# Two column halves for the last subtile, and a new order of loads, masks and attention items at the start of a fused attention and MLP kernel

## Chip, cores, metric

One Trainium2 chip, one core. The metric is the device time in microseconds (us) of one execution. Runs of a kernel mostly agree within 0.3 per cent; a few are in a slower state and left out of the ratios.

Names: TensorE (PE; PEld is its weight load), VectorE (DVE), ScalarE (ACT), GpSimd (POOL), SyncE (SP). A "q" after a name (PEldq, DVEq) marks that engine's sequencer, under which the profile lists branches, semaphore instructions and the issuing of DMAs; it can be ahead of the engine itself (in the kernel before, TensorE's reaches its branch at 305.5 us, and TensorE's last matmul ends at 308.97). A semaphore is a counter by which engines wait for one another. PSUM is the memory that the matmuls of this kernel write to; a bank is a part of it.

## The reference

```python
def reference(q, k, v, s, w_in, w_out):             # q, k, v: (8, 8, 576, 64)
    scores = q @ k^T / 8, causal mask, plus min(-(cum_i - cum_j), 0), cum = cumsum(max(s, 0))
    x = softmax(scores) @ v                          # -> (4608, 512): 8 batches of 576 tokens
    return gelu(x @ w_in) @ w_out                    # 512 -> 2048 -> 512, exact gelu
```

## The kernel before

The MLP runs over nine chunks of 512 tokens. A chunk has layer 1 (8 steps of two feature tiles; in the first chunk 16 steps, because its two token halves are done one after the other), then layer 2 in four subtiles of 128 tokens. The attention of the next batch is slotted in between. A filler is a matmul on zeros whose result nobody reads. A flag `bad`, computed from the data in an earlier chunk, decides whether a slow general path must redo everything; with this data it never does, but the branch is there. The last subtile of the last chunk is stored only behind the branch.

```python
    def l2_item(c, subs, f0=0, f1=FT, store=True):
        ...
        for ft in range(f0, f1):
            for sub in subs:
                nc.tensor.matmul(y_of[c, sub], lhsT=gT[:, ft, sub*128:(sub+1)*128],
                                 rhs=w_out_r[:, ft, :], start=(ft == 0), stop=(ft == FT - 1))
        if f1 == FT and store: ...                   # copy to SBUF, store
    ...
    load_v(0, nc.gpsimd, (0, 1)); load_w(0, 0); load_w(0, 1)      # one statement a line in the kernel
    load_v(0, nc.gpsimd, (2, 3)); load_w(0, 2); load_w(0, 3)
    scale_v(0, 1, nc.gpsimd)
    ...                                              # first scores, masks, attention items
            late = [                                 # what follows each of the 16 steps of chunk 0's layer 1
                [], [], [], [(av, 0, 0, 2), (av, 0, 1, 2)], [(av, 0, 0, 3)],
                [(av, 0, 1, 3), (to_xT, 0, 2, True)], [(to_xT, 0, 3, True)],
                [(scale_v, 0, 4), (av, 0, 0, 4)],
                [(av, 0, 1, 4), (to_xT, 0, 4, True)],
            ] + [[]] * 7
    ...
            for sub in range(4):                     # layer 2 of the last two chunks
                l2_item(c, (sub,), store=(c, sub) < LAST)
    fast.close()
    rv = nc.values_load(bad[0:1, 0:1], min_val=0, max_val=1)
    with tc.If(rv > 0):
        ...                                          # general path; ends with the last subtile anew
    with tc.manual_schedule():
        ...                                          # last subtile: columns 0:256 by VectorE, stored by SyncE,
                                                     # columns 256:512 by ScalarE, stored by ScalarE
```

Of the kernel before, what the change touches and what calls it, by code (L numbers as in the profile page):

```python
# [19 lines left out]
def kernel(  # L20
# [10 lines left out]
    nc = tc.nc  # L31
# [10 lines left out]
    ST = 5  # L42
# [195 lines left out]
        nc.scalar.activation(cum, s_pos, func=AF.Identity, scale=-1.0, bias=s_pos[:, 287:288])  # L238

    def weights():  # L240
        t_ps = ps.tile([128, ST, BH], fp32, tag="av", bufs=2, name="t_ps")
        for st in range(ST):
            n_st = 128 if st < ST - 1 else SL
            nc.tensor.transpose(
                t_ps[:n_st, st, :], cum[:, st * 128 : st * 128 + n_st], ident[:64, :64]
            )
        nc.scalar.activation(wb[:, 0 : ST - 1], t_ps[:, 0 : ST - 1], func=AF.Exp, scale=-1.0)
        nc.scalar.activation(wb[:SL, ST - 1], t_ps[:SL, ST - 1], func=AF.Exp, scale=-1.0)
# [46 lines left out]

    def cert_2():
        g = cg[0]
        g_ps = ps.tile([3, 128], fp32, tag="av", bufs=2, name="cg_ps")
        nc.tensor.transpose(g_ps, g, ident)
        g3 = const.tile([3, 1], fp32, name="cg3")  # L300
        nc.vector.tensor_reduce(g3, g_ps, axis=AX, op=ALU.max)

        cg[1] = g33 = const.tile([3, 3], fp32, name="cg33")
        nc.vector.tensor_scalar(g33, ident[:3, :3], g3, None, op0=MULT)

    def cert_3():
        g33 = cg[1]
        h_ps = ps.tile([64, 3], fp32, tag="av", bufs=2, name="ch_ps")
        nc.tensor.matmul(h_ps, lhsT=ones[:3, :64], rhs=g33, start=True, stop=True)
        h = const.tile([64, 3], fp32, name="ch")  # L310
        nc.vector.tensor_copy(h, h_ps)
        m = const.tile([64, 1], fp32, name="cm")
        nc.vector.tensor_tensor(m, h[:, 0:1], h[:, 1:2], op=MULT)

        f = const.tile([64, 1], fp32, name="cf")
        nc.vector.tensor_scalar(f, m, -2.0 * D * scale / 256, 1.0, op0=MULT, op1=ALU.add)
        nc.vector.tensor_scalar_max(f, f, 0.0)
        for _ in range(8):
            nc.vector.tensor_tensor(f, f, f, op=MULT)
        nc.vector.tensor_scalar(keep, keep, f, None, op0=MULT)  # L320
        nc.vector.tensor_tensor(goods[:, 6:9], drop, keep, op=ALU.is_le)
        le(goods[:, 9:10], m, MAX_SC / (D * scale))
        le(goods[:, 10:11], h[:, 2:3], 50.0**2)
        le(goods[:, 11:12], h[:, 2:3], 1e-6, ALU.is_ge)

    def cert_4():

        n_ps = ps.tile([1, 12], fp32, tag="av", bufs=2, name="cn_ps")
        nc.tensor.matmul(n_ps, lhsT=ones[:64, 0:1], rhs=goods, start=True, stop=True)
        n = const.tile([1, 1], fp32, name="cn")  # L330
        nc.vector.tensor_reduce(n, n_ps, axis=AX, op=ALU.min)
        le(n, n, 63.5)
        nc.vector.tensor_copy(bad, n)
# [67 lines left out]
    def to_xT(b, it, pe=False):  # L401
        n = 128 if it < ST - 1 else SL
        t0 = b * S + it * 128
        x = x_of[b, it]
        if not pe:
            nc.sync.dma_start_transpose(out=xT[:, :, t0 : t0 + n], in_=x[:n, :])
            return
        t_ps = ps.tile([128, NP, 128], bf16, tag="av", bufs=2, name="xt_ps")
        for p in range(NP):
            nc.tensor.transpose(  # L410
                t_ps[:, p, :n], x[:n, p * 128 : (p + 1) * 128], ident_bf[:n, :n]
            )
        nc.vector.tensor_copy(xT[:, :, t0 : t0 + n], t_ps[:, :, :n])  # L413
# [8 lines left out]

    def idle(n):

        f_ps = ps.tile([128, 256], fp32, tag="av", bufs=2, name="i_ps")
        for _ in range(n):
            nc.tensor.matmul(f_ps, lhsT=zero[:, :128], rhs=zero[:, :256], start=True, stop=True)

    def av_item(b, g, it, later=False):
        P = P_of[b, g]  # L430
        n = 128 if it < ST - 1 else SL
        o_ps = ps.tile([128, 4, D + 1], fp32, tag="av", bufs=2, name="av")
        for h in range(4):
            for i, (jt, off) in enumerate(BLK[it]):
                nc.tensor.matmul(  # L435
                    o_ps[:, h, :],
                    lhsT=P[:, h, off : off + 128],
                    rhs=vv[b % 2][:, jt, 4 * g + h, :],
                    start=(i == 0), stop=(i == len(BLK[it]) - 1),
                )  # L440
        if g == 0:
            x_of[b, it] = work.tile([128, H * D], bf16, tag="x", bufs=6, name="x")
        rc = work.tile([128, 4], fp32, tag="rc", bufs=3, name="rc")
        nc.vector.reciprocal(rc[:n], o_ps[:n, :, D])  # L444
        nc.vector.tensor_tensor(  # L445
            x_of[b, it][:n, g * 256 : g * 256 + 256].rearrange("p (h d) -> p h d", d=D),
            o_ps[:n, :, 0:D],
            rc[:n].unsqueeze(2).to_broadcast([n, 4, D]),
            op=MULT,
        )  # L450
        if g == HG - 1 and b > 0 and not later:
            to_xT(b, it)
# [20 lines left out]
            gT_of[c][:, f2 * 2 : f2 * 2 + 2, n0:n1], h_ps, func=AF.Gelu  # L473
        )

    def l2_item(c, subs, f0=0, f1=FT, store=True):
        gT = gT_of[c]
        if f0 == 0:
            for sub in subs:
# [1 line left out]
        for ft in range(f0, f1):  # L481
            for sub in subs:
# [1 line left out]
                    y_of[c, sub], lhsT=gT[:, ft, sub * 128 : (sub + 1) * 128], rhs=w_out_r[:, ft, :],  # L484
                    start=(ft == 0), stop=(ft == FT - 1),
                )
        if f1 == FT and store:
            for sub in subs:
                o_sb = ost.tile([128, KO * 128], fp32, tag="osb", bufs=3, name="o_sb")
                if c == 0:  # L490
                    nc.scalar.activation(o_sb, y_of[c, sub], func=AF.Copy)
                else:
                    nc.vector.tensor_copy(o_sb, y_of[c, sub])  # L493
                r0 = c * NB + sub * 128
                nc.sync.dma_start(out=out[r0 : r0 + 128, :], in_=o_sb)
# [24 lines left out]
    load_v(0, nc.gpsimd, (0, 1))  # L520
    load_w(0, 0)
    load_w(0, 1)
    load_v(0, nc.gpsimd, (2, 3))
    load_w(0, 2)
    load_w(0, 3)
    scale_v(0, 1, nc.gpsimd)
    load_v(0, nc.gpsimd, (4,))
    load_qks(1)
    load_w(1, 0)
# [14 lines left out]
    scale_v(0, 0)  # L544
    sc_first(1, 0, (1,), 0)
    av_item(0, 0, 0)
    av_item(0, 0, 1)
    mk_item(0, 1, 0, 0, 2)
    sc_first(0, 1, (1,))
    mk_item(0, 1, 0, 2, 4)  # L550
    sc_first(1, 1, (0,), 0)
    av_item(0, 1, 0)
    av_item(0, 1, 1)
    sc_first(1, 1, (1,), 0)
    to_xT(0, 0, True)
    filler(1)
    to_xT(0, 1, True)
    mk_item(0, 0, 1)
    scale_v(0, 2)
    mk_item(0, 1, 1)  # L560
    scale_v(0, 3)
    gelu_set()

# [6 lines left out]
    for c in range(NCH):  # L570
# [4 lines left out]
        if c == 0:  # L575

            late = [
                [], [], [], [(av, 0, 0, 2), (av, 0, 1, 2)], [(av, 0, 0, 3)],
                [(av, 0, 1, 3), (to_xT, 0, 2, True)], [(to_xT, 0, 3, True)],
                [(scale_v, 0, 4), (av, 0, 0, 4)],  # L580
                [(av, 0, 1, 4), (to_xT, 0, 4, True)],
            ] + [[]] * 7
            for half in range(2):
                for f2 in range(FT // 2):
                    l1_item(0, f2, half * 256, half * 256 + 256)
# [69 lines left out]
                    groups(c, (sub,), side[4 * sub : 4 * sub + 4])  # L655
        else:
            for sub in range(4):
                l2_item(c, (sub,), store=(c, sub) < LAST)
                if c == B - 1:
                    (cert_1, cert_2, cert_3, cert_4)[sub]()  # L660
    fast.close()
# [2 lines left out]
    with tc.If(rv > 0):  # L664
        with tc.tile_pool(name="gen", bufs=1) as gen, tc.tile_pool(
# [20 lines left out]
            with tc.For_i(0, B, 1) as b:  # L686
# [8 lines left out]
                for h in range(H):  # L695
# [17 lines left out]
                    for it in range(ST):  # L713
# [22 lines left out]
                        nc.vector.tensor_scalar(den[:n_i], den[:n_i], 1e-9, None, op0=ALU.add)  # L736
                        nc.vector.reciprocal(out=den[:n_i], in_=den[:n_i])
                        nc.vector.tensor_scalar(x[:n_i, :w], x[:n_i, :w], den[:n_i], None, op0=MULT)
                        o_ps = gps.tile([128, 128], fp32, tag="g3", bufs=1, name="go_ps")
                        e = h % 2  # L740
                        h0 = h - e
                        for jt in range(it + 1):
                            n_j = 128 if jt < ST - 1 else SL
                            p_ps = gps.tile([128, 128], fp32, tag="g1", bufs=2, name="gp_ps")
                            nc.tensor.transpose(
                                p_ps[:n_j, :n_i], x[:n_i, jt * 128 : jt * 128 + n_j], ident[:n_i, :n_i]
                            )
# [19 lines left out]
                        )  # L767
                    nc.scalar.activation(g[:, ft, :n], h_ps[:, :n], func=AF.Gelu)

            def layer_2(h_ps, g, sub):  # L770
                for ft in range(FT):
                    nc.tensor.matmul(
                        h_ps, lhsT=g[:, ft, sub * 128 : (sub + 1) * 128], rhs=w_out_r[:, ft, :],
                        start=(ft == 0), stop=(ft == FT - 1),
                    )

# [10 lines left out]
            g = gen.tile([128, FT, NB], bf16, name="gl")  # L787
            layer_1(g, (NCH - 1) * NB, NB)
            for sub in range(LAST[1], 4):
                layer_2(y_of[LAST[0], sub], g, sub)  # L790

    with tc.manual_schedule():
        for sub in range(LAST[1], 4):
            y = y_of[LAST[0], sub]
            r0 = LAST[0] * NB + sub * 128
            for i, (copy, eng) in enumerate(
                [(nc.vector.tensor_copy, nc.sync), (lambda o, a: nc.scalar.activation(o, a, func=AF.Copy), nc.scalar)]  # L797
            ):
                cols = slice(i * 256, i * 256 + 256)
                o_sb = ost.tile([128, KO * 128], fp32, tag="osb", bufs=3, name="o_sb")[:, :256]  # L800
                copy(o_sb, y[:, cols])  # L801
                eng.dma_start(out=out[r0 : r0 + 128, cols], in_=o_sb)


# [28 lines left out]
```

## Time and profile before

| | before |
|---|---|
| time, median of the first three runs | 316.21 us (315.69, 316.21, 320.75) |
| span of the profiled run, TensorE busy in it | 314.2 us, 302.0 us |
| layer 1 of the first chunk starts; layer 2 | 19.46; 36.74 us |
| last matmul ends | 308.97 us |
| VectorE's last copy starts; ScalarE's | 309.48; 309.94 us |
| last store issued (end of the issue) | 310.72 us |

The main lines of the profile before are shown in the prediction. Two more, from its chain of waits (who waited <- for what: us in total, times, longest):

```profile
ACT o_sb L797 <- DVE o_sb L801: 13.7, 1, 13.7
DVE o_sb L801 <- DVEq L664: 3.2, 1, 3.2
```

Line 664 is the branch. ScalarE's last copy waits for VectorE's, and VectorE's waits for its own sequencer at the branch.

### The profile page before, as it was taken

What the parts mean: (1) busy time and instruction counts of PE and PEld (TensorE: products, weight loads), DVE (VectorE), ACT (ScalarE), POOL (GpSimd) and SP (SyncE); (2) the same over time, 40 slices, a digit from 0 to 9 for tenths busy, and PEclk for the clock granted to TensorE, in tenths of its full rate; (3) what the DMA queues carried; (4) which work ended last, traced back from release to release, by engine and by line L of the source; (5) the groups of instructions that cost most, each with busy time, mean ns of one, the idle gap of its engine ahead of it and who ended that gap; (6) DMA issues with size and microseconds to landing.
All of it is one profiled execution on the core that took longest, in us unless ns stands there. A gap on an engine that the chain in (4) does not pass through costs nothing. (4 is left out here: it accounts for less than half of the span.)

```text
span 314.2 us, 6059 instructions
## 1 busy us (share of the span) xinstructions
PE 302.0 (96%) x2475; PEld 155.5 (49%) x2516; DVE 199.0 (63%) x398; ACT 191.0 (61%) x258; POOL 54.5 (17%) x73
## 2 busy tenths in 40 slices
PE   8899999999999999999999999999999999999993
PEld 3477755544554455545454455444544555444441
DVE  7776658599769856975598459955895532250020
ACT  2786878887737673875586658756776666105400
POOL 8653341133001500070007000500000000000000
PEclk9999999999999999999999999999999999999999
DMA  7999999779521973179307951633101331010012
GB/s 124 222 230 209 225 211 270 163 140 211 141 84 25 199 173 102 22 166 206 102 17 171 190 118 36 143 79 91 50 19 42 102 52 26 33 72 32 1 68 75
DMA packets 30979, 36.46 MB, mean 116 GB/s; under 512 B 15648, under 2 KB 20000, under 8 KB 30944
## 3 DMA queue, kind: packets, MB, share of 16 engines
q0 software_dynamic: 11552, 23.07, 38.1%
q1 hardware_dynamic: 19248, 12.80, 14.4%
q8 instruction: 21, 0.34, 0.4%
q14 instruction: 14, 0.11, 0.1%
q10 hardware_dynamic: 144, 0.13, 0.1%
HBM read 36.85 MB, written 9.44 MB: 147 GB/s over the span
## 5 line engine op out<-in xcount | busy, mean ns | idle before, releaser
L483 PE MATMUL o_ps<-w_out_r,gT 128*128 128x512 bf16 x551 | 132.2, 379 | 2.4 <-issue 1.6
L467 PE MATMUL h_ps<-xT,w_in_r 128*128 128x512 bf16 (+1 forms) x625 | 131.4, 357 | 1.3 <-DVE xT L413 0.5
L472 ACT ACTIVATE gT<-h_ps 128x1024 bf16<-128x1024 f32 (+1 forms) x80 | 75.1, 939 | 64.5 <-PE h_ps L467 63.7
L467 PEld LDWEIGHTS <-w_in_r 128*128 128x128 bf16 x640 | 59.8, 98 | 54.2 <-issue 0.6
L483 PEld LDWEIGHTS <-gT 128*128 128x128 bf16 x576 | 51.9, 98 | 56.6 <-issue 3.0
L359 ACT ACTIVATE P<-sc_ps 128x1024 bf16<-128x1024 f32 x56 | 54.3, 1021 | 30.5 <-PE sc_ps L344 30.5
L122 POOL DMA_DIRECT2D raw_v<-in_v_dram x40 | 34.1, 863 | 128.4 <-ACT sq L213 115.7
L493 DVE COPY o_sb<-o_ps 128x512 f32<-128x512 f32 x31 | 21.4, 691 | 46.5 <-PE o_ps L483 46.5
L444 DVE RECIPROCAL rc<-av 128x4 f32<-128x4 f32 (+1 forms) x80 | 14.0, 175 | 39.4 <-PE av L435 39.3
L187 DVE STREAM_TRANSPOSE qkT<-raw_qk 128x576 f32<-128x576 f32 x32 | 37.4, 1242 | 1.8 <-DMA raw_qk<-in_k_dram 1.7
L445 DVE TENSOR_TENSOR x<-av,rc 128x256 bf16<-128x256 f32 (+1 forms) x80 | 33.8, 423 | 3.0
L435 PEld LDWEIGHTS <-P 128*128 128x128 bf16 x576 | 27.1, 97 | 16.5 <-issue 0.8
L205 DVE TENSOR_REDUCE amx<-raw_qk 128x2 f32<-128x2304 bf16 x14 | 35.1, 2532 | 0.0
L435 PE MATMUL av<-vv,P 128*128 128x65 bf16 x576 | 30.5, 193 | 0.6 <-POOL vv L221 0.2
L367 DVE TENSOR_TENSOR P<-P,tri_bf 128x1024 bf16<-128x1024 bf16 (+1 forms) x33 | 22.0, 669 | 9.1 <-ACT P L359 9.1
L221 DVE TENSOR_TENSOR vv<-raw_v,wb 128x512 bf16<-128x512 f32 (+1 forms) x39 | 25.4, 690 | 2.5 <-DMA raw_v<-in_v_dram 2.5
L213 ACT ACTIVATE sq<-raw_v 128x512 bf16<-128x512 f32 (+1 forms) x40 | 24.8, 621 | 0.0
L344 PE MATMUL sc_ps<-qkT 32*128 32x256 bf16 (+2 forms) x560 | 18.2, 250 | 0.0
L344 PEld LDWEIGHTS <-qkT 32*128 32x128 bf16 x560 | 11.7, 92 | 12.4 <-issue 11.6
L498 ACT ACT_TABLE_LOAD x8 | 10.3, 1283 | 0.9 <-PEq L817 0.8
L419 PE MATMUL f_ps<-zero 128*128 128x512 bf16 x26 | 9.3, 494 | 1.2 <-DVE zero L150 1.2
L501 ACT ACT_TABLE_LOAD x8 | 10.3, 1283 | 0.1
(81 smaller groups left out, 92.3 us busy)
## 6 DMA issues: line engine op xcount, KB each, us to landing
out_dram<-o_sb SPq DMA_DIRECT2D x35, 256.0 KB, 2.2
raw_v<-in_v_dram POOLq DMA_DIRECT2D x32, 256.0 KB, 5.5
raw_qk<-in_q_dram POOLq DMA_DIRECT2D x7, 576.0 KB, 7.5
raw_qk<-in_k_dram POOLq DMA_DIRECT2D x7, 576.0 KB, 10.4
w_in_r<-in_moe_w_in_dram POOLq DMA_DIRECT2D x4, 512.0 KB, 12.1
w_out_r<-in_moe_w_out_dram POOLq DMA_DIRECT2D x4, 512.0 KB, 15.8
raw_v<-in_v_dram POOLq DMA_DIRECT2D x8, 128.0 KB, 6.4
raw_qk<-in_q_dram POOLq DMA_DIRECT2D x2, 288.0 KB, 6.2
```

The costliest lines, as they stand in the source:

```text
L122: eng.dma_start(out=t[:n_st, st, :, :], in_=bass.AP(tensor=v.tensor, offset=v.offset + b * H * S * D + st * 128 * D, ap=[[D, n_st], [S * D ...
L187: nc.vector.transpose(qkT[b % 2][:, i, g, :S, :].rearrange("p s e -> p (s e)").bitcast(fp32) .rearrange("p (l j) -> p j l", j=LT), raws[b, ...
L205: nc.vector.tensor_reduce(amx[:, b * HG + g], raws[b, "qk"][:, :, g, :], axis=AX, op=ALU.max, apply_absolute_value=True,)
L213: nc.scalar.activation(sq[:n_st], raws[b, "v"][:n_st, st].rearrange("p h d -> p (h d)"), func=AF.Square, accum_out=sumv[:n_st, b, st : st ...
L221: eng.tensor_tensor(vv[b % 2][:n_st, st, :, 0:D], raws[b, "v"][:n_st, st, :, :], w.unsqueeze(2).to_broadcast([n_st, H, D]), op=MULT,)
L344: nc.tensor.matmul(s_ps[h // 2][:, h % 2, off : off + n], lhsT=qk[r, 1, g, jt * 128 : jt * 128 + 128, e], rhs=qk[r, 0, g, i0 : i0 + n, e], ...
L359: nc.scalar.activation(P[:, 2 * h2 : 2 * h2 + 2, o : o + 512], s_ps[h2], func=AF.Exp, scale=scale)
L435: nc.tensor.matmul(o_ps[:, h, :], lhsT=P[:, h, off : off + 128], rhs=vv[b % 2][:, jt, 4 * g + h, :], start=(i == 0), stop=(i == len(BLK[it ...
L445: nc.vector.tensor_tensor(x_of[b, it][:n, g * 256 : g * 256 + 256].rearrange("p (h d) -> p h d", d=D), o_ps[:n, :, 0:D], rc[:n].unsqueeze( ...
L467: nc.tensor.matmul(h_ps[:, i, :], lhsT=w_in_r[:, ko, ft * 128 : (ft + 1) * 128], rhs=xT[:, ko, c * NB + n0 : c * NB + n1], start=(ko == 0) ...
L472: nc.scalar.activation(gT_of[c][:, f2 * 2 : f2 * 2 + 2, n0:n1], h_ps, func=AF.Gelu)
L483: nc.tensor.matmul(y_of[c, sub], lhsT=gT[:, ft, sub * 128 : (sub + 1) * 128], rhs=w_out_r[:, ft, :], start=(ft == 0), stop=(ft == FT - 1),)
```

## The change

The intent: let ScalarE and VectorE copy the two halves of the last subtile at the same time, from two PSUM banks; start attention items sooner; and take away the waits in the first layer 1 by moving attention items later, while w_in's third quarter lands ahead of value tiles 2 and 3.

```diff
+    def l2_last(c, sub):
+        y_of[c, sub] = []
+        for cols, tag in ((slice(0, 256), "mlp"), (slice(256, 512), "av")):
+            y = yps.tile([128, KO * 128], fp32, tag=tag, bufs=2, name="o_ps")[:, :256]
+            y_of[c, sub].append((cols, y))
+            for ft in range(FT):
+                nc.tensor.matmul(y, lhsT=gT_of[c][:, ft, sub*128:(sub+1)*128], rhs=w_out_r[:, ft, cols],
+                                 start=(ft == 0), stop=(ft == FT - 1))
...
     load_w(0, 1)
-    load_v(0, nc.gpsimd, (2, 3))
     load_w(0, 2)
-    load_w(0, 3)
     scale_v(0, 1, nc.gpsimd)
+    load_v(0, nc.gpsimd, (2, 3))
+    load_w(0, 3)
...
     av_item(0, 0, 0)
+    mk_item(0, 1, 0, 0, 2)
+    sc_first(0, 1, (1,), 0)
     av_item(0, 0, 1)
-    mk_item(0, 1, 0, 0, 2)
-    sc_first(0, 1, (1,))
...                                    # one filler moved; mk_item(0, 1, 1) ahead of scale_v(0, 2)
-                [], [], [], [(av, 0, 0, 2), (av, 0, 1, 2)], [(av, 0, 0, 3)],
-                [(av, 0, 1, 3), (to_xT, 0, 2, True)], [(to_xT, 0, 3, True)],
-                [(scale_v, 0, 4), (av, 0, 0, 4)],
-                [(av, 0, 1, 4), (to_xT, 0, 4, True)],
-            ] + [[]] * 7
+                [], [], [], [], [(av, 0, 0, 2)],
+                [(av, 0, 1, 2), (av, 0, 0, 3)], [(av, 0, 1, 3), (to_xT, 0, 2, True)],
+                [(to_xT, 0, 3, True)], [(scale_v, 0, 4), (av, 0, 0, 4)],
+                [(av, 0, 1, 4)], [(to_xT, 0, 4, True)],
+            ] + [[]] * 5
...
-                l2_item(c, (sub,), store=(c, sub) < LAST)
+                if (c, sub) < LAST: l2_item(c, (sub,))
+                else: l2_last(c, sub)
...                                    # tiles of tag "av" move to the pool that stays open; the general path
                                       # and the last copies take (columns, tile) pairs
```

More of the change, by code (lines that the diff above doesn't have):

```diff
@@ L240, in weights @@
     def weights():
-        t_ps = ps.tile([128, ST, BH], fp32, tag="av", bufs=2, name="t_ps")
+        t_ps = yps.tile([128, ST, BH], fp32, tag="av", bufs=2, name="t_ps")
         for st in range(ST):
@@ L297, in cert_2 @@
         g = cg[0]
-        g_ps = ps.tile([3, 128], fp32, tag="av", bufs=2, name="cg_ps")
+        g_ps = yps.tile([3, 128], fp32, tag="av", bufs=2, name="cg_ps")
         nc.tensor.transpose(g_ps, g, ident)
@@ L307, in cert_3 @@
         g33 = cg[1]
-        h_ps = ps.tile([64, 3], fp32, tag="av", bufs=2, name="ch_ps")
+        h_ps = yps.tile([64, 3], fp32, tag="av", bufs=2, name="ch_ps")
         nc.tensor.matmul(h_ps, lhsT=ones[:3, :64], rhs=g33, start=True, stop=True)
@@ L326, in cert_4 @@
     def cert_4():
-        n_ps = ps.tile([1, 12], fp32, tag="av", bufs=2, name="cn_ps")
+        n_ps = yps.tile([1, 12], fp32, tag="av", bufs=2, name="cn_ps")
         nc.tensor.matmul(n_ps, lhsT=ones[:64, 0:1], rhs=goods, start=True, stop=True)
@@ L407, in to_xT @@
             return
-        t_ps = ps.tile([128, NP, 128], bf16, tag="av", bufs=2, name="xt_ps")
+        t_ps = yps.tile([128, NP, 128], bf16, tag="av", bufs=2, name="xt_ps")
         for p in range(NP):
@@ L423, in idle @@
     def idle(n):
-        f_ps = ps.tile([128, 256], fp32, tag="av", bufs=2, name="i_ps")
+        f_ps = yps.tile([128, 256], fp32, tag="av", bufs=2, name="i_ps")
         for _ in range(n):
@@ L431, in av_item @@
         n = 128 if it < ST - 1 else SL
-        o_ps = ps.tile([128, 4, D + 1], fp32, tag="av", bufs=2, name="av")
+        o_ps = yps.tile([128, 4, D + 1], fp32, tag="av", bufs=2, name="av")
         for h in range(4):
@@ L474, in l1_item, with l2_item @@
         )
-    def l2_item(c, subs, f0=0, f1=FT, store=True):
+    def l2_last(c, sub):
[4 more added lines that the diff above has]
+            for ft in range(FT):
+                nc.tensor.matmul(
+                    y, lhsT=gT_of[c][:, ft, sub * 128 : (sub + 1) * 128], rhs=w_out_r[:, ft, cols],
+                    start=(ft == 0), stop=(ft == FT - 1),
+                )
+    def l2_item(c, subs, f0=0, f1=FT):
         gT = gT_of[c]
@@ L486, in l2_item @@
                 )
-        if f1 == FT and store:
+        if f1 == FT:
             for sub in subs:
@@ L522 @@
     load_w(0, 1)
+    load_w(0, 2)
+    scale_v(0, 1, nc.gpsimd)
     load_v(0, nc.gpsimd, (2, 3))
-    load_w(0, 2)
     load_w(0, 3)
-    scale_v(0, 1, nc.gpsimd)
     load_v(0, nc.gpsimd, (4,))
@@ L546 @@
     av_item(0, 0, 0)
+    mk_item(0, 1, 0, 0, 2)
+    sc_first(0, 1, (1,), 0)
     av_item(0, 0, 1)
-    mk_item(0, 1, 0, 0, 2)
-    sc_first(0, 1, (1,))
     mk_item(0, 1, 0, 2, 4)
     sc_first(1, 1, (0,), 0)
+    filler(1)
     av_item(0, 1, 0)
@@ L555 @@
     to_xT(0, 0, True)
-    filler(1)
     to_xT(0, 1, True)
     mk_item(0, 0, 1)
+    mk_item(0, 1, 1)
     scale_v(0, 2)
-    mk_item(0, 1, 1)
     scale_v(0, 3)
@@ L657 @@
             for sub in range(4):
-                l2_item(c, (sub,), store=(c, sub) < LAST)
+                if (c, sub) < LAST:
+                    l2_item(c, (sub,))
+                else:
+                    l2_last(c, sub)
                 if c == B - 1:
@@ L738 @@
                         nc.vector.tensor_scalar(x[:n_i, :w], x[:n_i, :w], den[:n_i], None, op0=MULT)
-                        o_ps = gps.tile([128, 128], fp32, tag="g3", bufs=1, name="go_ps")
+                        o_ps = gps.tile([128, 128], fp32, tag="g4", bufs=1, name="go_ps")
                         e = h % 2
@@ L743 @@
                             n_j = 128 if jt < ST - 1 else SL
-                            p_ps = gps.tile([128, 128], fp32, tag="g1", bufs=2, name="gp_ps")
+                            p_ps = gps.tile([128, 128], fp32, tag="g1", bufs=1, name="gp_ps")
                             nc.tensor.transpose(
@@ L768, in layer_1, with layer_2 @@
                     nc.scalar.activation(g[:, ft, :n], h_ps[:, :n], func=AF.Gelu)
-            def layer_2(h_ps, g, sub):
+            def layer_2(h_ps, g, sub, cols=slice(0, 512)):
                 for ft in range(FT):
                     nc.tensor.matmul(
-                        h_ps, lhsT=g[:, ft, sub * 128 : (sub + 1) * 128], rhs=w_out_r[:, ft, :],
+                        h_ps, lhsT=g[:, ft, sub * 128 : (sub + 1) * 128], rhs=w_out_r[:, ft, cols],
                         start=(ft == 0), stop=(ft == FT - 1),
@@ L789 @@
             for sub in range(LAST[1], 4):
-                layer_2(y_of[LAST[0], sub], g, sub)
+                for cols, y in y_of[LAST[0], sub]:
+                    layer_2(y, g, sub, cols)
     with tc.manual_schedule():
         for sub in range(LAST[1], 4):
-            y = y_of[LAST[0], sub]
             r0 = LAST[0] * NB + sub * 128
-            for i, (copy, eng) in enumerate(
-                [(nc.vector.tensor_copy, nc.sync), (lambda o, a: nc.scalar.activation(o, a, func=AF.Copy), nc.scalar)]
+            for (cols, y), copy, eng in zip(
+                y_of[LAST[0], sub],
+                (nc.vector.tensor_copy, lambda o, a: nc.scalar.activation(o, a, func=AF.Copy)),
+                (nc.sync, nc.scalar),
             ):
-                cols = slice(i * 256, i * 256 + 256)
                 o_sb = ost.tile([128, KO * 128], fp32, tag="osb", bufs=3, name="o_sb")[:, :256]
-                copy(o_sb, y[:, cols])
+                copy(o_sb, y)
                 eng.dma_start(out=out[r0 : r0 + 128, cols], in_=o_sb)
```

## The prediction

> **What bounds the kernel now.** I read the page first, then the matmul engine's timeline of the first 60 us, GpSimd's timeline (it issues the loads), the landing times of the loads by tile, and last the tail, including the sequencers. The page:
>
> ```profile
> span 314.2 us, 6059 instructions
> PE 302.0 (96%) x2475; PEld 155.5 (49%) x2516; DVE 199.0 (63%) x398; ACT 191.0 (61%) x258; POOL 54.5 (17%) x73
> DMA  7999999779521973179307951633101331010012
> ```
>
> TensorE is busy for 302.0 of 314.2 us; all that any reordering can win is in the other 12.2 us and in filler matmuls. Of these, 1.2 us lie before the first matmul, and 5.2 us after the last one ends (308.97). The third line says more: slices of 7.85 us, so for the first 50 us or so the DMA engines are full. The timeline of GpSimd shows what they are full of, and how each issue is held back by an earlier landing (start, duration, what ended the idle time):
>
> ```profile
> 12.14 0.75 POOL L147 DMA_DIRECT2D w_in_r<-in_moe_w_in_dram  x1 [0.77 <-DMA raw_qk<-in_k_dram]
> 14.05 1.10 POOL L221 TENSOR_TENSOR vv<-raw_v,wb 128x512 bf16<-128x512 f32 x1 [1.17 <-DMA raw_v<-in_v_dram]
> ...
> 26.11 1.55 POOL L147 DMA_DIRECT2D w_out_r<-in_moe_w_out_dram  x2 [1.95 <-DMA w_in_r<-in_moe_w_in_dram]
> ...
> 44.72 0.88 POOL L122 DMA_DIRECT2D raw_v<-in_v_dram  x1 [1.98 <-DMA w_out_r<-in_moe_w_out_dram]
> ```
>
> Counting issues, each one waits for the landing of the one eight before it. With the times from issue to landing I get the order of arrival: w_in quarters 0 and 1 at 16.1 and 18.7, value tiles 2 and 3 at about 19.8 and 20.8, w_in quarter 2 at 23.0 (10.61 + 12.4), quarter 3 at 25.84 (12.14 + 13.7), w_out quarter 2 at 41.0 (26.11 + 14.9), quarter 3 at 44.4 (about 26.9 + 17.5). Now the matmul engine at these moments:
>
> ```profile
> 25.66 0.39 PE L410 MATMUL xt_ps<-ident_bf,x 128*128 128x128 bf16 x4
> 25.88 1.04 PE L467 MATMUL h_ps<-xT,w_in_r 128*128 128x256 bf16 x8
> ...
> 28.25 0.37 PE L435 MATMUL av<-vv,P 128*128 128x65 bf16 x7 [0.20 <-DVE vv L221]
> ...
> 30.46 0.23 PE L410 MATMUL xt_ps<-ident_bf,x 64*128 64x64 bf16 x2 [0.56 <-DVE x L445]
> ...
> 44.57 1.03 PE L483 MATMUL o_ps<-w_out_r,gT 128*128 128x512 bf16 x4
> ```
>
> The step of layer 1 that needs w_in quarter 3 (the seventh, two feature tiles a step) starts at 25.88, 0.04 us after that quarter lands. The layer 2 group that needs w_out quarter 3 (the seventh of eight) starts at 44.57, some 0.15 us after its landing. So the head of this kernel is already in step with the stream of loads: TensorE shows almost no idle time there, but it has almost no room to be earlier either.
>
> The tail, from the rows of the branch that guards the general path, and the end of the timeline:
>
> ```profile
> L664 DVEq COMPARE_BRANCH  x1: 72/72/72, 306.2 to 306.2; - x1
> L664 SPq COMPARE_BRANCH  x1: 58/58/58, 306.7 to 306.7; - x1
> L664 DVEq EVENT_SEMAPHORE  x1: 21/21/21, 309.3 to 309.3; - x1
> ```
>
> ```profile
> 309.48 0.42 DVE L801 COPY o_sb<-o_ps 128x256 f32<-128x256 f32 x1 [3.23 <-DVEq L664]
> 309.94 0.38 ACT L797 ACTIVATE o_sb<-o_ps 128x256 f32<-128x256 f32 x1 [13.72 <-DVE o_sb L801]
> 309.94 0.34 SPq L802 DMA_DIRECT2D out_dram<-o_sb  x1
> 310.35 0.37 ACTq L802 DMA_DIRECT2D out_dram<-o_sb  x1
> ```
>
> VectorE branches at 306.2 and reaches the code behind the branch only at 309.3, 3.1 us later and after the last matmul. Its copy of the left half is held by the branch, not by TensorE. ScalarE branched long before (295.7), but waits for VectorE's copy to end, because both halves lie in one PSUM tile. The last store is therefore the one that ScalarE issues at 310.35.
>
> **What the Trainium skill says.** "PSUM — Partial Sum Buffer", section on PSUM bank collisions: two engines on one bank and quadrant must be kept apart, ScalarE and VectorE reads included. The trace agrees: 13.72 us of ScalarE's wait end with VectorE's copy. "Runtime: NRT & Kernel Launch", section "Instruction fetch mechanics": a taken branch out of the prefetch window costs a fetch. The trace fits that (3.1 us on VectorE, 2.6 on SyncE, 306.7 to 309.3) but does not name the fetch. "DMA: Bandwidth & Descriptors", section "Two DMAs through the same engine are not ordered": descriptors of one queue start in order but may finish out of it. The landings above came in order of issue. "TensorE: Matmul & The Clock Gate", section "Back-to-back issue gap": 262 cycles for 256 columns, 518 for 512; here 32 matmuls of 256 columns took 3.49 us (22.95 - 19.46), 0.109 us each.
>
> **The change part by part.**
>
> *Tail.* The last subtile's 16 matmuls of 512 columns (0.216 us each, 3.45 us) become 32 of 256 (0.109 each, 3.49 us): +0.04 us on TensorE, which ends near 309.0 less what the head won. VectorE's half is complete 1.75 us earlier, which buys nothing: its copy starts at 309.48 because of the branch. ScalarE's half, in its own bank, need not wait for VectorE; it starts at about 309.1 when the matmuls end and its store is issued at about 309.5. The last store is then SyncE's at 309.94, in place of ScalarE's at 310.35: -0.41 us, with 0.03 for the shorter issue -0.44.
>
> *Before layer 1.* One filler goes (0.22 us of TensorE) and another moves; the score matmuls of the sixth tile start about 0.4 us earlier, and ScalarE's gap of 0.37 us at 15.81 closes. But VectorE is a chain here: in the before trace its two mask pieces end at 16.93, then come two norms and two copies, to 19.40, and layer 1 starts at 19.46. The new order does norm, mask, norm, mask, so the second mask still ends at about 16.9. I expect layer 1 at 19.3 to 19.4.
>
> *Layer 1.* Quarter 2 now lands ahead of the value tiles, at about 21.1, these at about 22.2 and 23.2, and quarter 3, with the same bytes in front of it, again at 25.84. GpSimd now issues tiles 2, 3 and quarter 3 only after scaling value tile 1, from 15.1 to 17.7; the queue still holds quarters 1 and 2 until 21, so I expect no hole. Step 7 comes after six steps of 0.87 us and three attention items of 0.25 us, at 19.35 + 5.97 = 25.3: it waits half a microsecond for quarter 3 and starts at 25.9, as before, with one attention item and one transpose (0.48 us) not yet done. From there, before took 10.86 us to layer 2 (36.74), with about 1.0 us of stalls around 28.25 and 30.46. After: ten steps, 8.74; items and transposes 0.25 x 3 + 0.22 x 2 + 0.12 = 1.31; and one new stall, because the transpose of tile 3 now comes right before the first step of the second half, which reads it. Before, that transpose's copy began 0.42 us after it started and took 0.42, so the step waits about 0.9 - 0.22 = 0.68. Sum 10.73, a gain of 0.13 us.
>
> *Layer 2 of the first chunk.* It can be at most about 0.15 us earlier at the group of 44.57 before it waits for w_out quarter 3. So the head yields about 0.1 us, whatever happens before 44 us.
>
> After that TensorE is busy without a break (38.76 of 39.0 us from 270 to 309), and the gain is carried to the end. Sum: -0.44 - 0.10 = -0.54 us.
>
> **The rivals.** (1) The head pays in full. Adding the closed stalls (1.0), the filler (0.22) and an earlier start gives 1 to 1.4 us, hence 314.4 with the tail. For it: the idle times named in the trace do vanish in the new order. Against it: two arrivals pin the path. It needs the loads to land earlier. (2) The queue runs dry while GpSimd waits to scale tile 1 and everything behind comes later: each 0.1 us lost at quarter 3 or w_out is 0.1 us on the path, perhaps +0.5, and the tail is cancelled: 316.2. Against it: 1 MB or so is still queued at 15 us. (3) ScalarE's copy still waits for something of VectorE's (a buffer of the ring of three): then the tail yields nothing, 316.0. (4) The tail's store on SyncE is held by its own branch (309.3, then eight semaphores to 309.8) in all cases, so nothing more than 0.44 can come from there.
>
> **Range and chances.** The three runs of before were 315.69, 316.21 and 320.75, the profiled one 315.94. From 316.0, the middle of the undisturbed ones, -0.54 gives 315.5. Rivals 1 and 2 span 314.4 to 316.3, and the spread of single runs is a few tenths: 314.7 to 316.6. Two per cent are 6.3 us; nothing in this change can win that much out of 12.2 idle us, and no part adds it.
>
> **What would show it.** ScalarE's last copy before VectorE's, near 309.1, and SyncE's store last. A TensorE wait of about 0.5 us for w_in in front of layer 1's seventh step at 25.9, and one of 0.6 to 0.7 us on VectorE's copy of xT at about 28.3; no waits for scaled values or x. Layer 2 starting at 36.5 to 36.7. It is wrong if quarter 3 lands before 25.5 or after 26.2, if layer 2 starts before 36.2, or if ScalarE's copy still follows VectorE's.

## The result

The changed kernel takes 317.91 us (median of 6 runs, 317.34 to 318.92), the kernel before 315.63 (6 runs, one of them slow). The ratio of the fast runs is 1.0074, 95 per cent interval 1.0053 to 1.0094: slower by 0.7 per cent, clear of the noise, where 0.5 us faster was forecast. A ratio here is the mean time of one kernel's fast runs over that of the other's in the same rounds, so it is not quite the ratio of the medians quoted beside it.

Where does it come from? The timeline of the changed kernel's tail (start, duration, what ended the idle time):

```profile
305.39 3.66 PE L484 MATMUL o_ps<-w_out_r,gT 128*128 128x256 bf16 x32
305.59 0.69 DVE L506 COPY o_sb<-o_ps 128x512 f32<-128x512 f32 x1 [2.76 <-PE o_ps L496]
311.30 0.38 ACT L814 ACTIVATE o_sb<-o_ps 128x256 f32<-128x256 f32 x1 [15.05 <-PEq L680]
311.30 0.42 DVE L818 COPY o_sb<-o_ps 128x256 f32<-128x256 f32 x1 [5.02 <-PEq L680]
311.72 0.40 ACTq L819 DMA_DIRECT2D out_dram<-o_sb  x1
311.75 0.34 SPq L819 DMA_DIRECT2D out_dram<-o_sb  x1
```

The copies do run together, as intended. But both start at 311.30, though the matmuls end at 305.39 + 3.66 = 309.05. The releaser is PEq: TensorE's sequencer, at line 680, the branch. Its rows, first of the kernel before (the flag's load and the branch, lines 663 and 664), then of the changed one (679 and 680); after the duration in ns (shortest, median, longest) comes the first and last start in us:

```profile
L663 PEldq TENSOR_LOAD <-bad x1: 486/486/486, 304.9 to 304.9; - x1
L664 PEldq COMPARE_BRANCH  x1: 3642/3642/3642, 305.5 to 305.5; - x1
L664 PEldq EVENT_SEMAPHORE  x1: 51/51/51, 309.2 to 309.2; - x1
```

```profile
L679 PEldq TENSOR_LOAD <-bad x1: 755/755/755, 306.9 to 306.9; - x1
L680 PEldq COMPARE_BRANCH  x1: 3356/3356/3356, 307.8 to 307.8; - x1
L680 PEldq EVENT_SEMAPHORE  x1: 51/51/51, 311.2 to 311.2; - x1
L680 DVEq EVENT_SEMAPHORE  x1: 21/21/21, 309.6 to 309.6; - x1
```

TensorE's sequencer reached the branch at 307.8 instead of 305.5, with the matmuls ending at the same time (309.05 and 308.97). The branch takes it 3.4 to 3.6 us in both kernels. Before, that ended at 309.2, a moment before VectorE's own branch (309.3), so the profile named VectorE's. Now it ends at 311.2, and VectorE, free since 309.6, waits for it.

Why do the copies wait for an instruction behind the branch? The built program of the changed kernel (what the kernel is turned into before it runs; it isn't part of a trace) shows it. The general path would advance TensorE's semaphore by many steps, so the path that skips it has to advance it as well, and whoever stands behind the branch waits for the count after that:

```
TensorE, path not taken:  wait TensorE's count >= 2529, then add 592     -> 3121
VectorE, last copy:       wait TensorE's count >= 3120
ScalarE, last copy:       wait TensorE's count >= 3121
```

So no copy behind the branch can start before TensorE itself has passed the branch, however early its own half is complete. (In the kernel before TensorE's and VectorE's are the same but for the numbers; ScalarE's copy waits for VectorE's count there.)

What fills the 3.4 to 3.6 us? Both traces have one DMA packet of 16 KB of the kind "instruction" (queue q8 of the page) in that time: 306.54 to 307.69 before, 308.84 to 309.80 in the changed kernel, each 1.0 us after the branch began and 1.4 to 1.5 us ahead of the semaphore behind it. All thirteen kernels of this case with a branch have one such packet, from 1.0 to 1.6 us after TensorE's branch began. That fits a fetch of instructions by the branch; it is read from when things happen, and no run changes it by itself.

The head has the waits that were forecast, though not all at the forecast times. The matmul engine's timeline of the changed kernel:

```profile
18.74 4.53 PE L467 MATMUL h_ps<-xT,w_in_r 128*128 128x256 bf16 x40 [0.52 <-DVE xT L413]
...
25.34 1.05 PE L467 MATMUL h_ps<-xT,w_in_r 128*128 128x256 bf16 x8 [0.47 <-DMA w_in_r<-in_moe_w_in_dram]
...
28.47 1.05 PE L467 MATMUL h_ps<-xT,w_in_r 128*128 128x256 bf16 x8 [0.52 <-DVE xT L413]
...
41.55 1.89 PE L496 MATMUL o_ps<-w_out_r,gT 128*128 128x512 bf16 x7 [0.42 <-DMA w_out_r<-in_moe_w_out_dram]
```

The wait for w_in quarter 3 (0.47 us), the one for the transpose of tile 3 (0.52) and one for w_out (0.42) are there; layer 2 starts at 36.27 instead of 36.74. The w_out wait is at the group that needs quarter 2 (41.55), not at the one that needs quarter 3 (44.31 here). And from the start of layer 1 to layer 2 the changed kernel takes 17.53 us, the kernel before 17.28: the earlier layer 2 comes from the earlier start of layer 1, which differs from run to run (see experiment 4).

### The profile page after: what moved, and what is told of

Read it like the earlier page. It is cut to its first block, busy times and chain, and to the rows that moved or that the text cites. A ratio compares the mean times of both kernels' runs of the same rounds, so it can differ in the third digit from the quotient of the medians.

```text
span 316.2 us, 6091 instructions
## 1 busy us (share of the span) xinstructions
PE 301.2 (95%) x2490; PEld 156.6 (50%) x2531; DVE 199.3 (63%) x398; ACT 190.8 (60%) x258; POOL 54.3 (17%) x73
## 5 line engine op out<-in xcount | busy, mean ns | idle before, releaser
L496 PE MATMUL o_ps<-w_out_r,gT 128*128 128x512 bf16 x535 | 128.8, 379 | 2.8 <-issue 1.6
L496 PEld LDWEIGHTS <-gT 128*128 128x128 bf16 x560 | 50.3, 98 | 55.1 <-issue 3.5
## 6 DMA issues: line engine op xcount, KB each, us to landing
w_out_r<-in_moe_w_out_dram POOLq DMA_DIRECT2D x4, 512.0 KB, 16.1
```

The costliest lines, as they stand in the source:

```text
L496: nc.tensor.matmul(y_of[c, sub], lhsT=gT[:, ft, sub * 128 : (sub + 1) * 128], rhs=w_out_r[:, ft, :], start=(ft == 0), stop=(ft == FT - 1),)
```

## The experiments

All twelve kernels gave correct results and ran in three groups, each beside the kernel before on the same chip (medians 315.60, 315.59 and 315.66 us there).

**1. The head alone, the tail alone.** `head_only` is the changed kernel with the old tail, `tail_only` the kernel before with the new tail.

```diff
 head_only                                          tail_only
-                    l2_last(c, sub)                 (the start and the list `late` of the kernel before)
+                    l2_item(c, (sub,), store=False)
```

> The changed kernel's start and layer 1, with the old tail (16 matmuls of 512 columns into one tile, ScalarE after VectorE). Theory (branch): the loss of 2.3 us is all in the tail, where TensorE reaches its branch later because twice as many instructions stand before it, and both copies wait for TensorE's semaphore behind the branch. Then this kernel is at before minus the head's gain: layer 2 of the first chunk at 36.3 instead of 36.7, of which at most 0.3 us survives; 315.3 to 315.6 us, TensorE's branch at about 305.3, VectorE's last copy at 309.2 to 309.5. Rival (the head itself costs, for example by a fault in the middle of the kernel such as the wait at 186 us): 316.5 or more.

> The kernel before with only the new tail (two tiles in two banks, 32 matmuls of 256 columns). Branch theory: TensorE's branch near 307.9 instead of 305.5, its semaphore behind the branch near 311.4, both copies together right after it; 317.7 to 318.3 us, as the changed kernel plus what its head wins. Rival (head guilty): 315.2.

`head_only` took 315.69 us (314.78 to 316.86), ratio 1.0013 (0.9997 to 1.0029). `tail_only` took 318.03 us, ratio 1.0078 (1.0062 to 1.0095), with TensorE's branch at 307.6, its semaphore at 311.2 and both copies at 311.33. The whole loss is the tail's. The head wins nothing that these runs can tell (the median lies 0.1 us above the range that I gave for `head_only`).

**2. Number of instructions, or the second bank?** `one_bank` keeps the one tile in its one bank and only splits the columns; `mixed` splits 8 of 16 feature tiles, the last ones whole.

```diff
 one_bank
-        for ft in range(f0, f1):
+        for cols in (slice(0, 512),) if store else (slice(0, 256), slice(256, 512)):
+            for ft in range(f0, f1): ... y_of[c, sub][:, cols] ... w_out_r[:, ft, cols]
 mixed
+                half = not store and 0 < ft <= 8
+                for cols in (slice(0, 256), slice(256, 512)) if half else (slice(0, 512),): ...
```

> The kernel before with its last subtile computed as 32 matmuls of 256 columns, first the left half, then the right, both into the one tile in the one bank as before; the final copies as before. Branch theory (number of instructions ahead of the branch): TensorE's branch near 307.8, copies from 311.3 one after the other, 318.2 to 318.6 us, slower even than the changed kernel. Rival (the two tiles, their banks or the pool they come from bring a new wait): no loss, 315.6 us.

> The kernel before, with feature tiles 1 to 8 of its last subtile as two halves of 256 columns and the rest whole, all into the one bank: 24 matmuls instead of 16 or 32, the whole ones last. A dose between before and the one-bank run. Branch theory: the sequencer runs about 19 pairs of weights and matmul ahead of the array, here 8 x 0.216 + 11 x 0.109 = 2.9 us before the end instead of 4.1 and 2.15; TensorE's semaphore behind the branch comes about 1.2 us after the matmuls end (before 0.2, one bank 2.2); 316.3 to 316.8 us. Rival (a fixed cost of splitting, whatever the number): as the one-bank run, 317.6.

`one_bank` took 317.62 us, ratio 1.0072 (1.0056 to 1.0087): the loss is there without a second bank or another pool. In its profile the matmuls end at 304.82 + 3.66 = 308.48:

```profile
L665 PEldq COMPARE_BRANCH  x1: 3396/3396/3396, 307.2 to 307.2; - x1
L665 PEldq EVENT_SEMAPHORE  x1: 51/51/51, 310.7 to 310.7; - x1
```

I had expected it slower than the changed kernel, because its copies run one after the other. They do (310.77 and 311.22), but it is not slower. Its two stores, issued 0.42 us apart, landed 2.3 and 2.2 us after their issue; the two stores of the changed kernel, 0.03 us apart, took 2.8 and 2.6, those of `tail_only` 3.0 and 2.8. It looks as if the stores that go out together share their way and give back what the joint copies won. Since landings of 1.8 us occur in other runs, that is a reading, not a test.

`mixed`, whose matmuls end at 302.65 + 6.01 = 308.66, in its profile:

```profile
L665 PEldq TENSOR_LOAD <-bad x1: 483/483/483, 305.8 to 305.8; - x1
...
L666 PEldq COMPARE_BRANCH  x1: 3896/3896/3896, 306.4 to 306.4; - x1
L666 PEldq EVENT_SEMAPHORE  x1: 51/51/51, 310.3 to 310.3; - x1
```

The time at which TensorE loads the flag is the dose asked for: 2.9 us before the end of the matmuls (2.9 expected; the load starts at 305.805 in the packed trace), against 4.0 in the kernel before (304.937) and 2.1 in the changed one (306.941). In instructions the lead is the same. Counted in the traces, 17 matmuls and 16 weight loads start after that load in every one of the nine kernels that load the flag right before the branch. (The working in the expectation above ends at the right number by luck: it takes the last 8 matmuls as whole, but the edit leaves 7, feature tiles 9 to 15, and it takes 19 pairs from times that include what was already under way.) The branch then took 3.9 us, longer than the 3.4 I had counted on, so the copies came 1.8 us after the end of the matmuls (`one_bank` 2.3, before 0.5); the semaphore came 1.7 us after it instead of 1.2. The total, 317.51 us (316.93 to 319.68, the last at a granted clock of 0.982, near the 0.978 of the slow runs of before), missed the expected range and does not lie between: with the spread of these four runs the time doesn't show the dose, the trace does.

**3. Take the branch out of the way.** There are three degrees: `early_load` only loads the flag earlier, in the kernel before; `if_first` puts the branch of the changed kernel ahead of the last subtile; `no_branch` leaves the branch and the general path out (right for this data alone).

```diff
 early_load (and if_first)
+                if (c, sub) == (LAST[0], 1):
+                    rv = nc.values_load(bad[0:1, 0:1], min_val=0, max_val=1)
 if_first
-            gT_of[c] = work.tile([128, FT, NB], bf16, tag="gT", bufs=1, name="gT")
+            gT_of[c] = ost.tile([128, FT, NB], bf16, tag="gT", bufs=1, name="gT")   # outlives the branch
...            # general path: layer_1 writes gT_of[NCH - 1]; its own last subtile goes
     with tc.manual_schedule():
         for sub in range(LAST[1], 4):
+            l2_last(LAST[0], sub)          # both halves in tiles of tag "av"
```

> The kernel before, with the load of the branch's flag moved ahead of the second of the last four subtiles, so that no engine loads it right before the branch. Branch theory: TensorE's branch 0.5 us earlier (304.9 instead of 305.5), VectorE's at about 305.6 to 306.2, so the semaphores behind it come at or before the end of the matmuls (309.0), and VectorE's copy starts at 309.0 to 309.3 instead of 309.48: 0.1 to 0.4 us faster, 315.2 to 315.5 us. Rival (the copies wait for something else, such as SyncE's branch, or the last matmul itself plus a fixed latency): no change.

> The changed kernel without the flag's load, the branch and the general path behind it (right for this data alone, since the path is not taken). 32 matmuls in two banks as in the change. Branch theory: with no branch both copies start as the matmuls end, together, and the stores follow 0.45 us later: the last store is issued 0.9 us earlier than in the kernel before and 2.3 us earlier than in the changed one; 314.5 to 315.0 us. Rival (32 matmuls or the second bank cost by themselves): 317 or more.

> The changed kernel with the branch moved ahead of the last subtile: flag loaded before the second subtile of the last chunk, the general path writes the last chunk's gelu tile in place, and the last subtile's 32 matmuls into two free banks and its copies stand behind the branch. Branch theory: TensorE reaches the branch about 4 us before the third subtile's matmuls end, so its fetch is nearly hidden; it may lose 0.1 to 0.4 us because it waits behind the branch until its earlier matmuls are done. Copies start together at the end of the matmuls; 314.7 to 315.3 us, faster than both kernels. Rival (the fetch is not hidden, TensorE stands 3 us in front of the last subtile): 318.

`early_load`: 315.34 us, ratio 0.9986 (0.9972 to 1.0000); from the third subtile's copy to VectorE's last copy 3.55 us (305.92 to 309.47) where before took 3.93 (305.55 to 309.48). That is as expected, but the interval of the ratio ends at 1.0000.

`no_branch`: 314.20 us (313.94 to 314.24), ratio 0.9950 (0.9935 to 0.9966), a little better than the range given. Its tail:

```profile
305.29 3.66 PE L484 MATMUL o_ps<-w_out_r,gT 128*128 128x256 bf16 x32
...
307.24 0.42 DVE L688 COPY o_sb<-o_ps 128x256 f32<-128x256 f32 x1 [1.05 <-PE o_ps L484]
...
308.99 0.38 ACT L684 ACTIVATE o_sb<-o_ps 128x256 f32<-128x256 f32 x1 [12.83 <-PE o_ps L484]
```

Here the halves do what the change wanted: the left copy starts 1.75 us before the right one. (Of the other kernels `best_sub2` below alone does the same, 307.99 and 309.74.) So 32 matmuls and two banks cost nothing that shows here; the branch behind them costs.

`if_first`: 314.49 us (314.30 to 314.95), ratio 0.9963 (0.9949 to 0.9976). It beats both kernels, a little better than the range given. It keeps the general path in the program, but with this data no run takes that path, so the new version of it is untested. TensorE's rows and the two copies:

```profile
L679 PEldq COMPARE_BRANCH  x1: 3946/3946/3946, 301.2 to 301.2; - x1
L679 PEldq EVENT_SEMAPHORE  x1: 51/51/51, 305.3 to 305.3; - x1
...
308.50 0.42 DVE L814 COPY o_sb<-o_ps 128x256 f32<-128x256 f32 x1 [2.57 <-DVEq L679]
309.05 0.38 ACT L810 ACTIVATE o_sb<-o_ps 128x256 f32<-128x256 f32 x1 [13.14 <-SPq L679]
```

The branch passes while TensorE still works off the third subtile; the last subtile starts at 305.36, 0.11 us after that subtile's copy began, where in `no_branch` it starts 0.20 us before it (305.29 and 305.49). That 0.3 us is the price of waiting for TensorE's own count behind the branch. The left copy is still held, by VectorE's own branch, and starts only 0.55 us before the right one.

**4. The head's parts.** `loads_only` has only the new order of loads, `spread_only` only the new list `late`. `x3` is `head_only` with the items of tiles 2 and 3 pulled together, so that the transpose of tile 3 has a whole step to land.

```diff
 x3
-                [], [], [], [], [(av, 0, 0, 2)],
-                [(av, 0, 1, 2), (av, 0, 0, 3)], [(av, 0, 1, 3), (to_xT, 0, 2, True)],
-                [(to_xT, 0, 3, True)], ...
+                [], [], [], [], [(av, 0, 0, 2), (av, 0, 1, 2)],
+                [(av, 0, 0, 3), (av, 0, 1, 3)], [(to_xT, 0, 2, True), (to_xT, 0, 3, True)],
+                [], ...
```

> The kernel before with only the new order of loads (w_in quarter 2 and the scaling of value tile 1 ahead of the loads of tiles 2 and 3). Theory: the attention items of tile 2 after the fourth step now wait for the value tile, some 0.2 to 1 us, and tile 3 a step later likewise; quarter 3 lands as before, so the time is as before within 0.3 us: 315.4 to 315.9. Rival (the order of loads, with GpSimd held 5 us, delays all that comes behind): 316.2 or more.

> The kernel before with only the new places of the attention items of value tiles 2 to 4 in layer 1 (loads in the old order). Theory (pinned by arrivals): the fifth step now comes 0.5 us earlier and waits for w_in quarter 2, which still lands behind the value tiles, by 0.5 to 1.5 us; layer 2 starts at 36.5 to 37.3, the time is as before within 0.3 us: 315.4 to 315.9. Rival (spreading wins by itself): 315.0 or less.

> The run with the changed head and the old tail, with the attention items and the transposes of tiles 2 and 3 one step earlier in layer 1, so that the copy of xT has a whole step to land: it takes away the 0.5 us wait of the second half's first step. Theory (the arrivals of the weights pin the head): what is won there is waited for again at w_in quarter 3 or w_out quarters 2 and 3, and the time is as the head-only run and as before, 315.4 to 315.9. Rival (TensorE's own waits bound the head): 0.5 us less, 315.1.

`loads_only`: 316.26 us (315.39 to 317.75), ratio 1.0020 (1.0006 to 1.0034): a small loss, 0.06 us inside the rival's "316.2 or more". Its profile can't be compared, because that run, the slowest of the six, had a drop of the granted clock to 0.5 in the slice of 16 to 24 us. `spread_only`: 315.72 us, ratio 1.0012 (0.9998 to 1.0025): no gain, as expected. `x3`: 315.26 us (314.62 to 315.66), ratio 0.9984 (0.9970 to 0.9997). I had expected no gain; a small one is there.

Twelve of the profiles, those in the table, tell more than the times. The question is whether the head is pinned, that is, whether a start that comes earlier is waited away again because the weights arrive when they arrive. A marker that every kernel has is ScalarE's load of the gelu table in the first chunk's layer 2:

| head | layer 1 starts, us | marker, us | mean of the marker |
|---|---|---|---|
| old: before, early_load, tail_only, one_bank, mixed | 19.46, 19.37, 17.87, 17.83, 18.28 | 49.84, 50.23, 49.69, 49.31, 49.50 | 49.71 |
| new: changed, head_only, no_branch, if_first | 18.74, 17.77, 17.76, 18.92 | 49.59, 48.97, 49.53, 49.54 | 49.41 |
| new with x3's list: x3, best_late, best_sub2 (below) | 18.02, 18.14, 19.39 | 48.74, 48.85, 48.97 | 48.85 |

The first two columns show the pinning: layer 1 starts anywhere between 17.8 and 19.5 us, and at the marker this is nearly gone, because TensorE waits for weights in between (in `tail_only`, with an early start, 1.1 us for w_in; in `early_load`, with a late one, 0.6 us for w_out). But the pinning isn't complete: with x3's list, which removes a 0.5 us wait, the marker is 0.56 us earlier than with the new head alone. The 0.3 us between old and new head are weaker: the two groups overlap, and `spread_only`, which has the old order of loads and is not in the table, has the marker at 49.46.

Not all of that reaches the end. In the changed kernel the gain is 0.27 us until 184.75 us (185.02 before), and gone at 202.97 (202.93 before): the next chunk's layer 1, due at about 186.2, starts at 186.47. The second of the two transposes by DMA that it reads took 4.2 us to land there, 3.2 in the kernel before. The same 0.3 us is lost at this place in `no_branch`, `x3`, `best_late` and `best_sub2`, not in `head_only` and `if_first` (2.5 us to land), and in no kernel without the whole new head. The traces show what goes with the slow transposes: a 16 KB packet of the kind "instruction". In the five kernels that lose the 0.3 us it starts 1.7 us after the second transpose was issued (changed kernel: 183.95 after 182.21), and that transpose takes 4.1 to 4.2 us. In `head_only` and `if_first` it starts 3.5 us after it, when both have landed, and both take 2.5. In the seven kernels with the old head or a part of the new one it starts between 0.1 us before and 0.7 us after it, and the second takes 3.2 to 3.4 us, the first 3.8 to 4.3. No run moves that packet alone, so that it is the cause is likely but not shown.

**5. A version from these results.** `best_late` is `if_first` with x3's list. `best_sub2` moves the branch one subtile further ahead.

```diff
 best_sub2 (against best_late)
-                if (c, sub) < LAST:
+                if (c, sub) < (LAST[0], 2):
...
     with tc.manual_schedule():
+        l2_item(LAST[0], (2,))
         for sub in range(LAST[1], 4):
```

> The run with the branch ahead of the last subtile, with the earlier transposes of the x3 run in layer 1 as well. If the two gains add (0.35 and about 0.15 per cent): 314.0 to 314.4 us. If the head's gain is lost to the arrivals of the weights: as the branch-first run, 314.5.

> As the run before this one, with the branch one subtile earlier still, so that two subtiles stand behind it and the branches of VectorE (3 us) and SyncE (2.7 us) are over before the copies. Theory: the first half's store goes out at 1.5 us before the end of the matmuls and ScalarE's copy starts with their end: 0.1 us less than the run before, 313.9 to 314.3. Rival (TensorE stands longer at a branch placed earlier, because the copies of the subtile behind it are late): 0.3 us more.

`best_late` took 314.23 us (five of six runs 314.02 to 314.48, one slow), ratio 0.9961 (0.9947 to 0.9974): as good as `if_first`, on the median 0.3 us better, which the intervals don't tell apart. `best_sub2` took 314.41, ratio 0.9963 (0.9950 to 0.9976): no further gain, 0.1 us above the range given. Its profile shows why:

```profile
304.54 1.67 PE L496 MATMUL o_ps<-w_out_r,gT 128*128 128x512 bf16 x7 [1.03 <-issue]
```

With two subtiles behind the branch, TensorE stops for 1.03 us in the first of them, waiting for nothing that this view names. A 16 KB packet of the kind "instruction" is under way from 301.74 to 303.08, the next after that of the branch; whether TensorE waits for it is not shown.

## Why the prediction was wrong

*The failing step* is the tail's: "ScalarE's half, in its own bank, need not wait for VectorE; it starts at about 309.1 when the matmuls end". It started at 311.30, held by TensorE's own branch and not by VectorE. The term of -0.44 us was +1.40 us at the last store (end of issue 310.72 before, 312.12 after), and with slower landings +2.0 us in the span.

How it came about: I charged the split as time of the array, "+0.04 us on TensorE", which is right (3.66 against 3.45 + one matmul's drain; the end moved by 0.08). It also doubles the instructions, and TensorE's sequencer is ahead by a number of instructions (17 matmuls and 16 weight loads in these traces), not of microseconds: 4.0 us of whole matmuls, 2.1 of halves. I had the rows of the branch before me and read those of VectorE and SyncE, not TensorE's, whose semaphore came at 309.2, one tenth before VectorE's 309.3. "Its copy of the left half is held by the branch, not by TensorE" was true, by less than 0.1 us, and misleading: two waits ended at nearly the same time, and the profile names the last. None of the four rivals had TensorE's branch in it.

*That the early left half buys nothing* was right in result. The reason given (VectorE's own branch) was only one of three: both copies also wait for TensorE's branch, and in the built program of the changed kernel TensorE's count rises by 32 at the last matmul alone, so the left half has no signal of its own.

*Layer 1 starts at 19.3 to 19.4:* 18.74, but the start scatters by 1.7 us between runs of all kernels, so this says little.

*Waits of 0.5 us for quarter 3 and 0.68 for the transpose, layer 2 from 36.5 to 36.7:* 0.47, 0.52 and 36.27. The kind of the waits and their places in layer 1 were right, the transpose's was overestimated by 0.16, and layer 2 came earlier than the range. One of the prediction's own signs of being wrong came true: quarter 3 landed at 25.25 (16.25 + 9.0), before 25.5. But quarter 0, issued at the same time in both kernels, landed 0.65 us earlier too (15.45 against 16.1), so the whole start was early in this run. The wait for w_out came at quarter 2, not at quarter 3.

*"The head yields about 0.1 us, whatever happens before 44 us":* by the marker 0.3 us, with groups that overlap, by the time of `head_only` nothing that can be told (+0.0013, interval through zero). That w_out pins the path is too strong: x3's list got through.

*"The gain is carried to the end":* wrong in this run, it was given back at 186 us.

*The range* was too narrow by its own rivals: its lower end, 314.7, lies above the 314.4 of rival 1, and no rival was slower than 316.2.

## What to carry to other kernels

When a branch stands behind matmuls, count the instructions in front of it and not only their time: here matmuls of half the width cut the lead with which the sequencer came to the flag's load from 4.0 to 2.1 us. If the general path is rare, put the branch a few microseconds of matmuls ahead of the end, load its flag long before, and leave the last work behind it; that won 0.4 per cent here, and a step further ahead won no more. And where one wait is named, look for a second one that ended a tenth of a microsecond earlier: a change that removes or moves the first meets the second.

## What the Trainium skill lacked or had wrong

- "Runtime: NRT & Kernel Launch", "Instruction fetch mechanics": it says that a taken branch out of the prefetch window stalls, but gives no duration. Here TensorE's branch instruction lasted 3.4 to 3.9 us (3356 to 3946 ns in the rows shown), and the other sequencers took 2.4 to 3.4 us from the branch to the first instruction behind it (before: ScalarE 295.7 to 298.3, SyncE 306.7 to 309.3; changed: ScalarE 295.8 to 298.2, VectorE 306.2 to 309.6). A packet of the kind "instruction" lies inside TensorE's time in all thirteen kernels with a branch, so a fetch fits, but no run here isolates it.
- No page says that the lead of TensorE's sequencer is counted in instructions so that narrower matmuls shorten it. "TensorE: Matmul & The Clock Gate", "Back-to-back issue gap", has a 64-deep reorder window; here 17 matmuls and 16 weight loads (33 instructions) were still to start when the sequencer loaded the flag, in nine kernels alike.
- No page says that engines behind a skipped branch can wait for another engine to pass its own branch. Here both copies waited 2.2 us after the matmuls (309.05 to 311.30) for that alone.
- No page links the time of a DMA transpose to instruction packets. Here, at one place in fourteen traces, a transpose took 2.5 us with no such packet in its time and 3.2 to 4.3 us with one; no experiment isolates it.
- "TensorE: Matmul & The Clock Gate", "Back-to-back issue gap": its sustained figure of about 131 ns for 512 columns is not what this kernel gets; from one subtile's copy to the next (302.10 to 305.55) 16 matmuls took 3.45 us, 216 ns each, which is its formula for an isolated one.
